# One value run of four units a tile, with loads gated by sums of g

## The chip, the cores and the metric

The kernel runs on one core of a Trainium2 chip. The metric is device time in microseconds of the whole program; the lower the better. The core has five engines with queues of their own: TensorE (PE, matmuls and its weight loads), VectorE (DVE), ScalarE (ACT), GpSimd (POOL) and SyncE (SP, which here only issues DMAs). They run beside one another and wait for each other through semaphores; each takes its own instructions strictly in order, so an instruction that waits holds all behind it.

## The reference: what is computed

Sliding-window attention, then a two-layer MLP on its output:

```
scores = q @ k^T / 8, kept where |i - j| <= 32;  attn = softmax(scores);  x = attn @ v
h = x @ w_in;  g = h * sigmoid(1.702 * h);  out = g @ w_out
```

q, k and v are 8 batches x 8 heads x 576 positions x 64 (float32). x is 4608 tokens x 512, w_in 512 x 2048, w_out 2048 x 512, the output 4608 x 512 float32.

## The kernel before

**Units and tiles.** The 4608 tokens are cut into 36 units of 128 queries and 9 tiles of four units (512 tokens, `t` = 0 to 8). By "tile t" the text means the stretch of `front(t)` and `back(t)`: it does the MLP of units 4t to 4t+3 and, between its groups, the values (x) of units 4t+4 to 4t+7. A unit's queries are rows 128u+32 on; their windows lie in keys 128u to 128u+191, so a unit needs its own keys and the first 64 of the next unit's. `load_kq` and `load_v` (L141, L211) load a unit's queries, keys or values by DMA from POOL, cast to bfloat16; `T_dma` (L235) transposes queries and keys by DMA from SP (`turn(u)` does queries u and keys u+1). Values sit in `ve[u % 9]`; a second copy shifted by 64 rows, `vo`, is put together by two POOL copies (`odd_v`, L222; `spread` calls it). `vo` has five buffers, of which units from 16 on use three.

**Attention of a unit.** `scores` (PE) into two PSUM banks, exp on ACT, `band` (DVE) multiplies by the mask. `values(u, tag)` is 16 matmuls of 65 columns into two banks, four heads each; the 65th column is the sum of the weights. `norm` (L339, L340 on DVE) takes a reciprocal and a product for each bank, or both banks at once for the double bank "t"; `x_T` transposes the normed x into `xT`, by DMA from SP (L352), or on PE (L356) if it is given a bank.

**The MLP of a tile.** Both layers use seven block products in place of eight (a Strassen scheme): sums of blocks of x (`x_sums`), of w_in and w_out (made once) and of g (`g_sums`, four DVE operations per group) are the operands. Layer 1 of a tile is four groups `n` = 0 to 3 (`l1_group`). Each works in the four single banks A, C, B, E: products 1 (into A) and 7 (into C), ACT copies both, products 6 and 2, DVE adds (L484, "the first sum"), products 5 and 4, DVE adds (L490, "the second sum"), product 3; four gelus on ACT (L471) empty the banks. Between the products, `fill(1)`, `fill(7)`, `fill(2)` and `fill(4)` issue matmuls of layer 2 (list `l2`, tiles behind) from the table SHARES; they are what PE does while DVE and ACT work. Product 5 waits for the first sum, product 3 for the second. `side` and `fill(4)` hand DVE the masks and the sums of g of the group before. Layer 2 has its own banks LA and LB.

**Order.** Everything is issued in one hand-written order (`opening`, `run`, then for each tile `front(t)` and `back(t)`); there is no scheduler. `front(t)` does the scores of the four units of tile t+1, the last sums of g and the sums of x of tile t. `back(t)` does tile t's four groups and, between them, the values of tile t+1. With u = 4t+4 the unit that the next tile begins with, `back` before:

- in tile 2: four value runs of one unit, two in front of groups 1 and 3 and two inside them (bank "t" each time);
- in tiles 3 to 7: in front of group 1 the values of u (banks A, C) and u+1 (bank "t"), in front of group 3 those of u+2 and u+3 likewise; norms and the DMA transposes of x follow each run; AHEAD says how many layer-2 matmuls stand around a run;
- in every group: `turn(u+n+4)`, `fetch(u+n+5)` (queries, keys and values of one unit each) and `spread(u+n+2)`, with shifts in tile 3;
- unit 34's x is transposed on PE in `front(8)`, the others by DMA.

The loads have no gate of their own: POOL issues each as soon as it gets there and the buffer is free (five stages each for queries and keys). POOL is slowed by the odd-value copies, which wait for PE's values and for landed loads.

## Time and profile before

| | us |
|---|---|
| median of 3 runs | 281.32 (281.23 to 282.04) |
| the profiled execution, its own time | 281.27 |
| its span (first to last instruction) | 279.5 |
| PE busy | 268.2 (96%) |
| DVE busy | 210.9 (75%) |
| ACT busy | 195.4 (70%) |
| POOL busy | 133.0 (48%) |

Times in the profile are microseconds from the span's start. Lines of code are given as L70 and so on; L70 is the helper that records every matmul, so matmuls are told apart by their tiles: `pv` values, `sc` scores, `h` layer 1, `o` layer 2, `tp` transposes. A row of the timeline gives start, duration, engine, line, operation, tiles written and read, shapes and a count; matmuls are pipelined, so a row's duration is longer than its share of PE, and the distance between starts tells what PE spends. In a row of DMA issues the last number is the median time from issue to landing. The stretches that tiles 2 to 7 take in the trace begin at 78.9 (tile 2's group 0) and, with the scores in `front`, at 100.4, 128.0, 155.7, 183.3 and 210.9; the last layer-2 work ends the program.

### The profile page before, as it was taken

How to read it: one execution, taken by the hardware profiler on the slowest of the kernel's cores; microseconds unless marked ns; L12 is line 12 of the kernel's file. 1: busy time of each engine (PE TensorE's matmuls, PEld its weight loads, DVE VectorE, ACT ScalarE, POOL GpSimd, SP SyncE). 2: the span in 40 equal slices, each digit the busy share in tenths (PEclk: the TensorE clock that was granted, in tenths of full speed). 3: DMA queues.
4: the chain of work that ended last, by engine and by line, in shares of the span. 5: the costliest groups of instructions: out<-in, count | busy, mean ns of one | idle time of the engine just before them, and what ended most of it. 6: DMA issues, size and time to landing. Idle time of an engine off the chain costs nothing.

```text
span 279.5 us, 8854 instructions
## 1 busy us (share of the span) xinstructions
PE 268.2 (96%) x3632; PEld 222.6 (80%) x3632; DVE 210.9 (75%) x491; ACT 195.4 (70%) x343; POOL 133.0 (48%) x199
## 2 busy tenths in 40 slices
PE   1989999999999999999999999999999999999995
PEld 1568656776888888888888888888888888888884
DVE  3454598897997798788888887888778887945731
ACT  2586893989897588758875877687759775568411
POOL 8894695999593554635684519442520100000000
PEclk9999999999999999999999999999999999999999
DMA  8999999999999999999999999999972050202023
GB/s 88 166 204 199 178 207 165 185 136 159 131 167 140 203 120 140 172 189 115 182 194 178 126 163 159 134 183 132 168 91 85 2 115 19 77 2 75 2 104 124
DMA packets 150265, 37.61 MB, mean 135 GB/s; under 512 B 138064, under 2 KB 145872, under 8 KB 150224
## 3 DMA queue, kind: packets, MB, share of 16 engines
q0 software_dynamic: 106656, 18.42, 95.5%
q1 hardware_dynamic: 43120, 18.10, 37.9%
q8 instruction: 28, 0.46, 0.7%
q10 hardware_dynamic: 448, 0.52, 0.6%
q14 instruction: 13, 0.11, 0.1%
HBM read 36.83 MB, written 9.44 MB: 166 GB/s over the span
## 4 chain that ended last, share of the span: by engine, by line
PE 90%; DMA 4%; POOL 3%; ACT 1%; issue 1%; POOLq 0%
PE o L70 41%; PE h L70 39%; PE pv L70 4%; DMA w<-in_moe_w_in_dram 4%; PE sc L70 3%; POOL ve L211 1%; POOL kq L152 1%; PE tp L201 1%; PE tp L244 1%; ACT p L279 1%; POOL w L125 1%; PE tp L368 0%; ACT kq L67 0%; PE tp L356 0%; ACT L692 0%
## 5 line engine op out<-in xcount | busy, mean ns | idle before, releaser
L471 ACT ACTIVATE g<-h 128x512 f16<-128x512 f32 x128 | 72.2, 598 | 35.0 <-PE h L70 34.8
L222 POOL COPY vo<-ve 64x264 int32<-64x264 int32 x71 | 32.7, 461 | 79.3 <-PE pv L70 52.0
L70 PEld LDWEIGHTS <-g 128*128 128x128 f16 x576 | 54.5, 98 | 10.1
L70 PE MATMUL h<-xs,a 128*128 128x256 f16 x384 | 57.6, 272 | 0.0
L70 PEld LDWEIGHTS <-a 128*128 128x128 f16 x512 | 49.5, 98 | 9.1
L70 PE MATMUL o<-w,g 128*128 128x256 f16 (+1 forms) x320 | 55.0, 294 | 0.0
L70 PEld LDWEIGHTS <-w 128*128 128x128 f16 x496 | 47.7, 98 | 7.6 <-DMA w<-in_moe_w_in_dram 0.2
L70 PE MATMUL h<-xT,w 128*128 128x256 f16 (+1 forms) x368 | 53.5, 277 | 0.1
L70 PEld LDWEIGHTS <-gs 128*128 128x128 f16 x384 | 36.7, 98 | 4.7
L70 PE MATMUL o<-b,g 128*128 128x256 f16 x256 | 38.3, 273 | 0.0
L70 PE MATMUL o<-b,gs 128*128 128x256 f16 x256 | 37.7, 273 | 0.0
L484 DVE TENSOR_TENSOR h<-h,s 128x512 f32<-128x512 f32 x32 | 22.4, 699 | 19.8 <-PE h L70 19.1
L211 POOL DMA_DIRECT2D ve<-in_v_dram x40 | 34.3, 864 | 5.6 <-DMA w<-in_moe_w_out_dram 2.1
L279 ACT ACTIVATE p<-sc 128x512 bf16<-128x512 f32 x64 | 32.8, 618 | 1.2 <-PE sc L70 1.0
L67 ACT COPY h<-h 128x512 f32<-128x512 f32 x32 | 18.8, 588 | 16.7 <-PE h L70 16.3
L340 DVE TENSOR_TENSOR x<-pv,rec 128x256 f16<-128x256 f32 (+1 forms) x52 | 27.4, 527 | 1.8
L141 POOL DMA_DIRECT2D qst<-in_q_dram x35 | 28.2, 809 | 0.3
L490 DVE TENSOR_TENSOR h<-h,s 128x512 f32<-128x512 f32 x32 | 22.4, 699 | 6.4 <-PE h L70 6.1
L141 POOL DMA_DIRECT2D kst<-in_k_dram x31 | 26.5, 855 | 0.8 <-DMA w<-in_moe_w_out_dram 0.8
L309 DVE TENSOR_TENSOR p<-p,mask 128x1024 bf16<-128x1024 bf16 x32 | 22.3, 696 | 0.2
L67 ACT COPY s<-h 128x512 f32<-128x512 f32 x32 | 19.2, 600 | 1.2
L70 PE MATMUL h<-xs,w 128*128 128x256 f16 x128 | 19.2, 273 | 0.0
(88 smaller groups left out, 343.2 us busy)
## 6 DMA issues: line engine op xcount, KB each, us to landing
out_dram<-o_sb SPq DMA_DIRECT2D x33, 256.0 KB, 4.6
ve<-in_v_dram POOLq DMA_DIRECT2D x32, 128.0 KB, 6.9
kst<-in_k_dram POOLq DMA_DIRECT2D x25, 128.0 KB, 6.5
qst<-in_q_dram POOLq DMA_DIRECT2D x21, 128.0 KB, 5.6
w<-in_moe_w_out_dram POOLq DMA_DIRECT2D x4, 512.0 KB, 11.0
w<-in_moe_w_in_dram POOLq DMA_DIRECT2D x3, 512.0 KB, 9.9
qst<-in_q_dram POOLq DMA_DIRECT2D x7, 96.0 KB, 5.7
kq<-in_q_dram POOLq DMA_DIRECT2D x2, 256.0 KB, 5.9
```

The costliest lines, as they stand in the source:

```text
L67: (eng.copy if eng is self.nc.scalar else eng.tensor_copy)(out, in_)
L70: self.nc.tensor.matmul(out, lhsT, rhs, start=start, stop=stop, skip_group_check=True)
L125: self.nc.gpsimd.dma_start(self.w1[:, :, lo:lo + n], self.w_in[:, lo:lo + n].rearrange("(k p) f -> p k f", p=128))
L141: self.nc.gpsimd.dma_start(t[off:off + n], src[b, :, s:s + n, :].rearrange("h s d -> s h d"))
L211: self.nc.gpsimd.dma_start(t[off:off + n, :, :self.D], self.v[b, :, s:s + n, :].rearrange("h s d -> s h d"))
L222: eng.tensor_copy(*((words(vo[64:128]), words(self.ve[u % 9][64:128])), (words(vo[0:64]), words(nxt)))[i])
L279: self.nc.scalar.activation(p[:, eo].rearrange("k h s -> k (h s)"), sc[eo], AF.Exp, scale=self.scale)
L309: (eng or self.nc.vector).tensor_mul(pv, pv, msk.to_broadcast([128, 8, 2, SQ]))
L340: dve.tensor_mul(x[:, 4 * at:4 * (at + n), :].rearrange("p (b h) d -> p b h d", b=n), acc[:, :, :, :D], r.to_broadcast([128, n, 4, D]))
L471: act.activation(g[:, f, 256 * half:256 * half + 256], bank.rearrange("p (i n) -> p i n", i=2), AF.Gelu_apprx_sigmoid)
L484: dve.tensor_add(e, b, s7)
L490: dve.tensor_add(c, b, s7)
```

## The change

- **Values and norms.** In tiles 2 to 7 `values_four(u)` does all four units in one run of 64 matmuls in front of group 2. The 32 heads lie one behind the other in five stretches: A (7 heads), E (7, put at the end of the bank, with the first matmul of each half widened over what lies ahead of them), C (4), and the two halves of "t" (7 each). `norm_four` norms A, C and E right behind the run (then the transposes of x of units u and u+1 are issued), one layer-2 matmul goes ahead of group 2, and the halves of "t" are normed in that group's two `side` places, each followed by one transpose of x. x lies in one fixed buffer of four units (`xn`). Groups 1 and 3 have no value run any more; unit 34's x goes by DMA too. All four masks of a tile are handed out from group 0 on.
- **Shares.** SHARES is new and AHEAD is gone; the sum over a tile is the same 112 with `front`, and 64 over tile 2's groups as before.
- **Loads.** Behind groups 2 and 3 of tile 2 and all groups from tile 3 on, as long as there are loads, POOL does a copy of one element of the sums of g (`seen`), of the group before. POOL's loads behind it wait for that sum. In tile 2 queries and keys 17 to 19 come without a gate, values 17 and 18 and queries 20 (keys 21) behind group 2, values 19 and 20 behind group 3. From tile 3's group 2 on each group loads unit u+n+7.
- **Odd values.** Units from 16 on use four `vo` buffers (2, 3, 4, 0 in turn); the copies for u+2 and u+3 are made behind group 0, for u+4 and u+5 behind groups 2 and 3.
- **Transposes of queries and keys.** Tile t issues `turn` u+5 and u+6 in group 0, u+7 in group 1 and u+8 in group 3; tile 3 issues units 20 to 23 in groups 0 and 1 and 24 in group 3, so that keys 24 (in `turn(23)`) are ahead of the four x made in it (units 16 to 19) on SP's queue; tile 2 issues 16 to 19 in groups 0 to 2.

```diff
@@ -94,7 +94,9 @@
         self.v_first = cst.tile([64, self.H, 66], BF16, name="v_first")
         self.ve = [cst.tile([128, self.H, 66], BF16, name=f"ve{i}") for i in range(9)]
         self.vo = [cst.tile([128, self.H, 66], BF16, name=f"vo{i}") for i in range(5)]
+        self.xn = cst.tile([128, 4, self.H, self.D], F16, name="xn")
         self.spark = cst.tile([128, 1], F32, name="spark")
+        self.seen = cst.tile([1, 1], F16, name="seen")
 
     def setup_mask(self):
 
@@ -210,9 +212,12 @@
         for off, b, s, n in list(self.pieces(128 * u, 128))[which]:
             self.nc.gpsimd.dma_start(t[off:off + n, :, :self.D], self.v[b, :, s:s + n, :].rearrange("h s d -> s h d"))
 
+    def odd(self, u):
+        return self.vo[u % 5 if u < 16 else (2, 3, 4, 0)[u % 4]]
+
     def odd_v(self, u, eng, parts=(0, 1)):
 
-        vo = self.vo[u % (3 if u > 15 else 5)]
+        vo = self.odd(u)
         nxt = self.v_first if u == self.NU - 1 else self.ve[(u + 1) % 9][0:64]
 
         def words(ap):
@@ -322,14 +327,14 @@
         for h in range(self.H):
             o = slice((h % 4) * (D + 1), (h % 4 + 1) * (D + 1))
             for blk in range(2):
-                vt = (self.ve[u % 9], self.vo[u % (3 if u > 15 else 5)])[blk]
+                vt = (self.ve[u % 9], self.odd(u))[blk]
                 w = p[:, h % 2, h // 2 * 2 + blk, :] if len(p.shape) == 4 else p[:, h % 2, h // 4, h // 2 % 2, blk, :]
                 self.mm(acc[h // 4][64 * blk:64 * blk + 64, o], w, vt[:, h, :D + 1],
                         start=(h % 4 == 0))
 
     def norm(self, u):
         dve, D = self.nc.vector, self.D
-        x = self.x[u] = self.sb("x", [128, self.H, D], F16, 4)
+        x = self.x[u] = self.xn[:, u % 4]
         rec = self.sb("rec", [128, 2, 4, 1], F32, 3)
         at = 0
         for acc in self.acc.pop(u):
@@ -340,6 +345,42 @@
             dve.tensor_mul(x[:, 4 * at:4 * (at + n), :].rearrange("p (b h) d -> p b h d", b=n), acc[:, :, :, :D],
                            r.to_broadcast([128, n, 4, D]))
             at += n
+
+    FOUR = {"A": 0, "E": 7, "C": 14, "t0": 18, "t1": 25}
+
+    def four(self, tag):
+        return self.FOUR[tag], 4 if tag == "C" else 7, 512 - 7 * (self.D + 1) if tag == "E" else 0
+
+    def values_four(self, u):
+
+        D = self.D
+        p = [self.p.pop(u + i) for i in range(4)]
+        b = {tag: self.bank(tag, name="pv") for tag in "AECt"}
+        self.acc[u] = b | {"t0": b["t"][:, 0], "t1": b["t"][:, 1]}
+        for tag in self.FOUR:
+            lo, n, pad = self.four(tag)
+            for i in range(n):
+                x, h = divmod(lo + i, self.H)
+                at, more = pad + i * (D + 1), pad * (i == 0)
+                for blk in range(2):
+                    vt = (self.ve[(u + x) % 9], self.odd(u + x))[blk].rearrange("p h d -> p (h d)")
+                    self.mm(self.acc[u][tag][64 * blk:64 * blk + 64, at - more:at + D + 1],
+                            p[x][:, h % 2, h // 2 * 2 + blk, :], vt[:, h * (D + 2) - more:h * (D + 2) + D + 1],
+                            start=(i == 0))
+
+    def norm_four(self, u, tags, units):
+
+        dve, D = self.nc.vector, self.D
+        x = self.xn.rearrange("p u h d -> p (u h) d")
+        for tag in tags:
+            lo, n, pad = self.four(tag)
+            acc = self.acc[u].pop(tag)[:, pad:pad + n * (D + 1)].rearrange("p (h e) -> p h e", e=D + 1)
+            r = self.sb("rec4", [128, 7, 1], F32, 3)[:, 0:n]
+            dve.reciprocal(r, acc[:, :, D:])
+            dve.tensor_mul(x[:, lo:lo + n], acc[:, :, :D], r.to_broadcast([128, n, D]))
+        for i in units:
+            self.x[u + i] = self.xn[:, i]
+            self.x_T(u + i)
 
     def x_T(self, u, tag=None, eng=None):
         nc = self.nc
@@ -603,11 +644,8 @@
 
 
 
-    SHARES = {("first", 1): (3, 0, 5, 4), ("first", 2): (0, 6, 6, 6), ("first", 3): (3, 1, 7, 7), ("last", 0): (0, 12, 6, 6),
-              0: (4, 4, 6, 6), 1: (3, 3, 6, 6), 2: (0, 6, 5, 6), 3: (2, 2, 5, 5)}
-
-
-    AHEAD = {1: (0, 6), 3: (2, 3)}
+    SHARES = {("first", 0): (2, 4, 5, 3), ("first", 1): (2, 3, 5, 4), ("last", 0): (0, 12, 6, 6),
+              0: (4, 5, 6, 7), 1: (4, 5, 6, 7), 2: (2, 4, 5, 7), 3: (3, 4, 5, 5)}
 
     def opening(self):
 
@@ -733,13 +771,18 @@
         self.x_T2(6, "t", dve)
         self.do(self.l2, 6)
 
+    def ahead(self, what, *us):
+        for u in us:
+            if "q" in what:
+                self.load_kq("q", u)
+                self.load_kq("k", u + 1)
+            if "v" in what:
+                self.load_v(u)
+
     def fetch(self, u):
         self.load_kq("q", u)
         self.load_kq("k", u + 1)
-        if u < 16:
-            self.load_v(u + 1)
-        elif u >= 18:
-            self.load_v(u - 1)
+        self.load_v(u + 1)
 
     def spread(self, u):
         if 16 <= u < self.NU:
@@ -761,7 +804,6 @@
             self.l2eng = self.nc.scalar
             do(late, 3)
             do(l2, 8)
-            self.x_T(self.NU - 2, "t", self.l2eng)
             xs = self.x_sums(t)
             do(xs, 1)
             do(l2, 12)
@@ -788,60 +830,62 @@
         do, l2 = self.do, self.l2
         u = 4 * t + 4
         bands = [lambda i=i: self.band(u + i) for i in range(4)] if more else []
-        dv = bands[0:2]
+        dv = bands
         for n in range(4):
-            if (t, n) == (3, 1):
-                self.turn(20)
-            if (t, n) != (3, 0):
-                self.turn(u + n + 4)
-            if (t, n) not in ((2, 3), (3, 0), (3, 3)):
-                self.fetch(u + n + 5)
-            if t == 2 and n in (1, 3):
-                self.values(u + n - 1, "t")
-                self.norm(u + n - 1)
-                self.x_T(u + n - 1)
-            elif more and n in (1, 3):
-                do(l2, self.AHEAD[n][0])
-                self.values(u + n - 1, "AC")
-                self.norm(u + n - 1)
-                if u + n < self.NU - 1:
-                    self.x_T(u + n - 1)
-                self.values(u + n, "t")
-                self.norm(u + n)
-                self.x_T(u + n)
-                do(l2, self.AHEAD[n][1])
-            if (t, n) == (3, 0):
-                self.fetch(20)
-            self.spread(u + n + 2)
-            if (t, n) == (3, 0):
-                self.fetch(21)
-            if (t, n) == (3, 3):
-                self.fetch(24)
-
-            key = ("first", n) if t == 2 else ("last", n) if not more else n
+            for i in {2: ((4,), (5,), (6, 7), ()), 3: ((4, 5), (6, 7), (), (8,))}.get(t, ((5, 6), (7,), (), (8,)))[n]:
+                self.turn(u + i)
+            if t == 2:
+                self.ahead("kq", *((17,), (18, 19), (), ())[n])
+            if more and n == 2:
+                self.values_four(u)
+                self.norm_four(u, ("A", "C", "E"), (0, 1))
+                do(l2, 1)
+
+            key = n if more else ("last", n)
+            if t == 2:
+                key = ("first", n) if n < 2 else n
             share = dict(zip((1, 7, 2, 4), self.SHARES.get(key, (3, 3, 5, 5))))
 
             def fill(i):
                 do(l2, share[i])
                 self.l2eng = self.nc.scalar
-                if t == 2 and n in (1, 3) and i == 7:
-                    self.values(u + n, "t")
-                    if n == 3:
-                        self.norm(u + n)
-                        self.x_T(u + n)
-                if i == 4:
-                    do(dv, 2 if (t, n) == (2, 2) else 99)
+                if i == 4 or more and (n, i) == (1, 7):
+                    do(dv, 99 if i == 4 else 2)
 
             def side(i):
-                if (t, n, i) == (2, 1, 0):
-                    self.norm(u + n)
-                    self.x_T(u + n)
+                if more and n == 2:
+                    self.norm_four(u, (f"t{i}",), (2 + i,))
                 else:
                     do(dv, 1)
 
             self.l1_group(t, n, fill, side)
-            dv += bands[2:4] if n == int(t == 2) else []
             dv += self.g_sums(t, 2 * n, 2)
+            if more and (t > 2 or n > 1):
+                if u + n + 7 <= self.NU:
+                    c = 2 * ((n - 1) % 4) + 1
+                    self.nc.gpsimd.tensor_copy(self.seen, self.gs[t - (n == 0)][0:1, 2, c, 255:256])
+                if t == 2:
+                    if n == 2:
+                        self.ahead("v", 17, 18)
+                        self.ahead("kq", 20)
+                    else:
+                        self.spread(16)
+                        self.ahead("v", 19, 20)
+                        self.ahead("kq", 21)
+                    continue
+                if (t, n) == (3, 0):
+                    self.ahead("kq", 22)
+                    self.spread(17)
+                for i in ((2, 3), (), (4,), (5,))[n]:
+                    self.spread(u + i)
+                if (t, n) == (3, 0):
+                    self.ahead("v", 21, 22)
+                    self.ahead("kq", 23)
+                elif (t, n) == (3, 1):
+                    self.ahead("v", 23)
+                    self.ahead("kqv", 24)
+                else:
+                    self.ahead("kqv", u + n + 7)
         return dv
 
     def run(self):
@@ -897,7 +941,7 @@
         self.seed2 = dve
         self.odd_v(14, pool)
         self.odd_v(15, pool)
-        self.fetch(16)
+        self.ahead("kq", 16)
         late = self.back(2)
         for t in range(3, self.NT):
             self.front(t, late)
```

## The prediction

> **What bounds the kernel now.** I read the page's head first, then the busy times by stretch, then TensorE (PE) row by row.
>
> ```profile
> span 279.5 us, 8854 instructions
> PE 268.2 (96%) x3632; PEld 222.6 (80%) x3632; DVE 210.9 (75%) x491; ACT 195.4 (70%) x343; POOL 133.0 (48%) x199
> DMA  8999999999999999999999999999972050202023
> 128.73:156.36 27.63, 27.63 (x385) 23.90 (x386) 23.30 (x55) 20.68 (x37) 16.87 (x26) 1.00 2.30 168
> ```
>
> The last row is tile 4's stretch: length, then PE, PEld, DVE, ACT, POOL. A tile takes 27.63 us and PE is busy in all of it at full clock; only what PE issues, and what it waits for, can move the end. The DMA engines are as full until 75% of the span, so a late transfer is the danger. The profiled execution took 281.27 us, 0.05 under the median of 281.32; I sum against 281.27.
>
> Where PE is not packed shows in the start times. Tile 4's two value runs (its pairs of units), in order of time:
>
> ```profile
> 137.70 0.60 PE L70 MATMUL h<-xT,a 128*128 128x256 f16 x4
> 138.23 0.22 PE L70 MATMUL pv<-ve,p 128*64 128x65 bf16 x1
> 138.28 0.20 PE L70 MATMUL pv<-ve,p 128*64 128x65 bf16 x1
> 138.76 0.19 PE L70 MATMUL pv<-vo,p 128*64 128x65 bf16 x1
> 138.89 0.83 PE L70 MATMUL o<-w,g 128*128 128x256 f16 x6
> 149.96 0.19 PE L70 MATMUL pv<-vo,p 128*64 128x65 bf16 x1
> 150.10 0.19 PE L70 MATMUL pv<-ve,p 128*64 128x65 bf16 x1
> 238.92 0.60 PE L70 MATMUL o<-w,gs 128*128 128x256 f16 x4
> 239.36 0.39 PE L356 MATMUL tp<-identh,x 128*128 128x128 f16 x4
> 239.58 0.60 PE L70 MATMUL o<-w,gs 128*128 128x256 f16 x4
> ```
>
> A 256-column matmul takes 0.11 (four from 238.92 to 239.36). Four from 137.70 end at 138.14, and the run begins at 138.23: entering costs 0.09. Its 32 matmuls start within 0.53, about 0.017 each, with a slow first pair (+0.02). Leaving takes 0.13 from 138.76, 0.11 over one matmul. So one run's changeover costs 0.22. In the second run the ninth matmul comes 0.14 after the eighth (149.96 to 150.10): 0.12 of waiting for bank C. The rest of the tile is back to back but for known waits of 0.04.
>
> **The change, part by part.**
>
> *Values, tiles 3 to 7.* Two runs of 32 become one of 64: the same matmuls, one changeover less (-0.22). The new run takes banks A, E, C, t in turn and reaches C after 28 matmuls (0.48) instead of 8; the wait of 0.12 on C's gelu goes. Two matmuls into E are 57 columns wider: +0.03.
>
> What is late next is the norm. The run lies right before group 2, whose first product writes bank A again, with one layer-2 matmul between.
>
> ```profile
> 138.59 0.18 DVE L339 RECIPROCAL rec<-pv 128x4 f32<-128x4 f32 x1 [0.16 <-PE pv L70]
> 138.81 0.42 DVE L340 TENSOR_TENSOR x<-pv,rec 128x256 f16<-128x256 f32 x1
> 139.93 0.69 DVE L340 TENSOR_TENSOR x<-pv,rec 128x512 f16<-128x512 f32 x1
> 86.61 0.70 DVE L484 TENSOR_TENSOR h<-h,s 128x512 f32<-128x512 f32 x1 [1.36 <-PE h L70]
> 87.22 0.20 DVE L339 RECIPROCAL rec<-pv 128x8 f32<-128x8 f32 x1
> 87.45 0.69 DVE L340 TENSOR_TENSOR x<-pv,rec 128x512 f16<-128x512 f32 x1
> 88.06 0.69 DVE L490 TENSOR_TENSOR h<-h,s 128x512 f32<-128x512 f32 x1
> 88.99 0.42 DVE L67 COPY o<-o 128x256 f32<-128x256 f32 x1
> 89.32 0.41 DVE L67 COPY s7o<-o 128x256 f32<-128x256 f32 x1
> 88.23 0.60 PE L70 MATMUL o<-b,g 128*128 128x256 f16 x4
> 88.80 0.49 PE L70 MATMUL h<-xT,a 128*128 128x256 f16 x3
> ```
>
> The reciprocal starts 0.23 after the start of the bank's last matmul (the eighth, about 138.36, to 138.59). Bank A now has 14: last start 0.25, reciprocal at 0.48, 0.20 long (0.18 for 4, 0.20 for 8), a gap of 0.04, and a product of 448 elements, 0.62 between the rows of 256 (0.42) and 512 (0.69): 1.34, with 0.05 until PE goes on (88.06+0.69 to 88.80) 1.39. PE is there after 64x0.017=1.09, 0.11 to leave and 0.11 for one matmul: 1.31. Wait: +0.08.
>
> In the same group the t bank's first norm lies between the group's two sums on DVE, as a norm lies in tile 2 above: there the sums start 1.45 apart (86.61, 88.06), and PE with four matmuls of cover (88.23) waits 0.13 (88.67 to 88.80). New: 0.61 to the reciprocal, 0.20+0.04+0.54 for the norm (a product's end overlaps the next by 0.08), and layer 2's own 256-element sum, 0.33 as between 88.99 and 89.32: 1.72 apart, 0.27 more, against seven matmuls of cover, 0.33 more: +0.07. The second t norm and the four sums of g end before group 3 needs DVE.
>
> Per tile -0.22-0.12+0.03+0.08+0.07 = -0.16; five tiles **-0.8**. Bounds: both waits gone, -0.31 a tile; one 256-element step (0.33) more ahead of each, +0.50. I take the middle: DVE's order around the run is the one worked out.
>
> *Tile 2.* Four runs of one unit become one: -3x0.22, +0.03+0.08+0.07. Its group 0 loses cover: three layer-2 matmuls ahead of the last product, five now.
>
> ```profile
> 82.52 0.70 DVE L490 TENSOR_TENSOR h<-h,s 128x512 f32<-128x512 f32 x1
> 83.30 0.38 PE L70 MATMUL h<-xT,a 128*128 128x256 f16 x2
> ```
>
> With two fewer that product would come at 83.08, but the sum ends at 83.22: +0.19. Group 1 keeps four, and its 0.13. Sum **-0.3**.
>
> *Unit 34's x by DMA, not PE.* Four transposes less, 239.36 to 239.58: **-0.2**. Its ACT copy goes too, beside other work. Its transpose is issued in group 2, one group and 4 us before it is read.
>
> *Loads, gates, odd values.* POOL gains 16 one-element copies; each holds the loads behind it until a sum of g is done. Data for a tile then still lands a tile ahead of its scores (the q, k loaded behind group 0 are transposed in group 1 and read in the next tile), so I cost the holding itself at nothing; where that cover is thin is the next part. New in tiles 4 to 7: four odd-value copies now open on the last sum of g, just where DVE makes the sums of x.
>
> ```profile
> 128.78 0.42 DVE L412 TENSOR_TENSOR gs<-g 128x512 f16<-128x512 f16 x1
> 129.05 0.42 POOL L222 COPY vo<-ve 64x264 int32<-64x264 int32 x1
> 129.23 0.51 DVE L413 TENSOR_TENSOR g<-g 128x512 f16<-128x512 f16 x1
> ```
>
> The sum that began inside a POOL copy took 0.51, not 0.42; the one that began first took 0.42. Three sums stand ahead of product 6, 0 to 0.27 late at 0.09 each; that product gets one layer-2 matmul more of cover (0.11), so PE waits 0 to 0.16. I take +0.03 in each of four tiles, near the low end, since only sums that begin inside a copy are lengthened: **+0.1**. [...]
>
> *x of tile 3 behind keys 24.* On SP, queries 23 and keys 24 are now transposed ahead of the four x made in tile 3 (units 16 to 19, summed in front of tile 4), and they are loaded late: on POOL behind the odd values of unit 19, which wait for values 20, loaded after the gate in tile 2's group 3.
>
> ```profile
> ve<-in_v_dram POOLq DMA_DIRECT2D x32, 128.0 KB, 6.9
> kst<-in_k_dram POOLq DMA_DIRECT2D x25, 128.0 KB, 6.5
> L211 POOL DMA_DIRECT2D ve<-in_v_dram x40 | 34.3, 864 | 5.6 <-DMA w<-in_moe_w_out_dram 2.1
> 123.78 2.51 SPq L352 DMA_TRANSPOSE xT<-x  x2
> 156.08 0.43 DVE L415 TENSOR_TENSOR gs<-g,gs 128x512 f16<-128x512 f16 x1
> 155.66 0.70 PE L70 MATMUL sc<-qT,kT 64*64 64x64 bf16 x48
> 133.00 0.43 DVE L400 TENSOR_TENSOR xs<-xT 128x512 f16<-128x512 f16 x1 [0.40 <-DMA xT<-x]
> 133.77 0.60 PE L70 MATMUL h<-xs,a 128*128 128x256 f16 x4
> DMA to landing us min/median/max: 4.6/5.3/7.8
> DMA to landing us min/median/max: 4.3/6.8/9.4
> ```
>
> The last rows are x's transposes in 100 to 164 us and the q, k transposes in 100 to 130. Now the last x is issued at 125.0, lands by 133.0 and is 0.40 late for DVE, hidden from PE. New, step by step: the gate opens with the last sum of g of tile 2's group 2. In tile 4 that sum ends at 156.51, 0.85 behind the next scores (155.66); two tiles of 27.63 earlier and 0.3 gained, 100.9. Unit 16's odd copies (0.9), then values 19 and 20, issued by 102.7 and landed 6.9 later, 109.6. Until 109.9 POOL issues q21, k22, q22, k23 (0.86 each, an estimate of 1.4 in two pieces) and copies for units 17 and 18; unit 19's are done by 110.8; v21, v22 and q23 bring k24's issue to 114.0, landed 120.5. Its transpose and a store (1.3, and 0.8 by estimate) last to 122.6; three x (1.26 each) put the last issue at 126.4, landed at 131.7 to 134.2. It is needed by 133.77 less 0.48 for the sum and 0.46 gained by then: 132.8. Wait 0 to 1.4; a landing near the middle, 133.0, gives 0.2 and the longer tail speaks for a little more: **+0.3**. With values 20 and keys 24 at 9.4 it is 4.
>
> Sum: -0.8-0.3-0.2+0.1+0.3 = -0.9: **280.4 us**.
>
> **Rivals.** *Slower: tile 3's x (above).* It decides alone: gains without it are 1.2, so a wait of 2.0 passes +0.3% (0.84 us, about what a measurement here can tell from no change). For it: loads that bunch up behind gates, the 9.4 of the row above; against it: the idle DMA that the gates leave before. At a wait of 3: 283.1.
>
> [...]
>
> *No change.* The changeovers are saved and DVE takes them back: at one of the two places in each of six tiles it is 0.2 later than worked out, as when a POOL copy holds one of its steps: 280.4+1.2=281.6. For it: neither place has cover left; against it: DVE idles in between.
>
> *More.* x lands in time and the two waits on DVE vanish, -0.31x5-0.4-0.2: 279.1. For it: DVE is busy in 23.30 of 27.63; against it: both waits are chains of dependent steps, not a full engine.
>
> **How the numbers follow.** Forecast 0.42 (its own range 279.8 to 280.7), more 0.10, no change 0.23, x of tile 3 0.18, lock 0.07. The bound of 0.3% lies at 280.5, inside the forecast's own range: four fifths of it (0.34) and all of *more* make 0.44 faster; the rest of the forecast and *no change* 0.31 the same; the two slower ones 0.25. The range of 279.2 to 282.8 leaves out the lock, the far end of tile 3's x and the edge of *more*.
>
> **What would show it.** In the changed profile: one run of 64 values a tile, PE's first product 0.2 after it, no wait inside it; tile period 27.4 to 27.5 from tile 4 on; sums of x without DMA waits except in front of tile 4; no transposes at the end. It is wrong if PE idles in the layer-1 groups behind DVE's norms, if the run waits for odd values or values, or if tile 4's first group waits for x.

## The result, and the profile after

The changed kernel takes 288.4 us (median of 6 runs, 287.13 to 289.32) against 281.39 for the kernel before on the same chip (281.23 to 282.22): 1.0238 times, with a 95% interval of 1.0207 to 1.0269. The forecast was 280.4, in a range of 279.2 to 282.8. The profiled execution took 289.32, the longest of the six; its mean granted clock was 0.982, that of the other five 0.988. In the runs below, executions more than 1.5% above the fastest of their kernel (two of ten in each of two runs) are left out of medians, ratios and intervals.

The page of the changed kernel: its span, and the slices of PE and of its granted clock.

```profile
span 287.6 us, 8849 instructions
PE   1989999999999999994799999999999999999994
PEclk9999999999999999998589999999999999999999
```

PE has a hole in slices 19 and 20 (129 to 144 us), and its clock falls there. Everything else is packed as before. The next two fences cut both kernels into tiles, from the first scores of one to those of the next: length, PE, PEld, DVE, ACT, POOL, and then the granted clock (third number from the end). First the kernel before, for tiles 2, 3, 4 and for 7 with the tail, then the changed kernel for the same, with tile 5 and a stretch inside tile 4.

```profile
65.94:100.39 34.45, 34.45 (x568) 27.86 (x567) 28.17 (x66) 27.09 (x49) 20.42 (x30) 1.00 1.87 160
100.39:128.03 27.64, 27.64 (x386) 23.98 (x385) 23.51 (x57) 20.59 (x36) 16.88 (x24) 1.00 1.54 153
128.03:155.66 27.63, 27.63 (x385) 23.90 (x384) 23.30 (x56) 20.68 (x37) 16.87 (x26) 1.00 2.28 168
210.94:275.85 64.91, 64.91 (x728) 57.35 (x728) 44.65 (x106) 38.96 (x72) 0.81 (x2) 1.00 0.19 56
```

```profile
65.66:99.81 34.15, 34.12 (x568) 27.87 (x568) 29.03 (x70) 26.86 (x49) 16.42 (x24) 1.00 1.67 148
99.81:127.22 27.41, 27.41 (x385) 23.89 (x384) 23.08 (x54) 20.77 (x37) 22.54 (x36) 1.00 2.11 140
127.22:164.16 36.94, 31.20 (x385) 25.43 (x384) 22.70 (x54) 20.94 (x37) 15.06 (x26) 0.86 1.44 156
164.16:191.58 27.42, 27.42 (x385) 23.88 (x385) 22.70 (x54) 20.78 (x37) 16.43 (x28) 1.00 1.68 154
219.00:283.47 64.47, 64.47 (x724) 57.03 (x724) 44.27 (x104) 38.55 (x71) 0.00 (x0) 1.00 0.18 59
136.03:145.40 9.37, 7.41 (x35) 5.00 (x36) 3.56 (x8) 3.04 (x4) 1.15 (x2) 0.51 1.72 186
```

Tile 2 gains 0.30, tile 3 0.23, tiles 5 and 6 0.22 each, tile 7 with the tail 0.44. Tile 4 alone takes 36.94, where 27.42 stood to be had: +9.52. What it waits for stands in its timeline (start, duration, engine, line, operation; in brackets the idle time and its releaser):

```profile
131.66 0.60 PE L70 MATMUL o<-w,g 128*128 128x256 f16 x4
136.03 1.01 PE L70 MATMUL h<-xT,w 128*128 128x256 f16 x4 [3.77 <-DMA xT<-xn]
136.84 1.06 PE L70 MATMUL o<-w,g 128*128 128x256 f16 x4
139.86 1.03 PE L70 MATMUL h<-xs,a 128*128 128x256 f16 x4 [1.96 <-DVE xs L441]
...
139.38 0.43 DVE L441 TENSOR_TENSOR xs<-xT 128x512 f16<-128x512 f16 x1 [7.58 <-DMA xT<-xn]
```

By the starts (four matmuls from 131.66 end at 132.1, four from 136.84 at half clock at 137.7) PE idles 3.9 for the first transposed x of tile 3 and 2.2 for the sum of x behind the last. Then it runs at half clock: in the stretch of 9.37 the granted clock is 0.51, and four matmuls take 0.83 (136.03 to 136.84) instead of 0.44. That is the rest, 3.4.

The queues that lead to it, from the same timeline, and then, by tile, the landing of keys 24 (issue to landing in us) and the four transposes of x (durations of the issues in ns, first and last start, landing):

```profile
109.70 3.84 POOL L227 COPY vo<-ve 64x264 int32<-64x264 int32 x6
115.71 0.91 POOL L143 DMA_DIRECT2D qst<-in_q_dram  x1
116.59 0.92 POOL L143 DMA_DIRECT2D kst<-in_k_dram  x1
...
124.49 1.19 SPq L240 DMA_TRANSPOSE kT<-kst  x1
125.79 1.00 SPq L546 DMA_DIRECT2D out_dram<-o_sb  x2
126.89 6.84 SPq L393 DMA_TRANSPOSE xT<-xn  x4
```

```profile
DMA to landing us min/median/max: 7.9/7.9/7.9
...
L393 SPq DMA_TRANSPOSE xT<-xn x4: 1188/1398/2206, 126.9 to 132.5; - x4
DMA to landing us min/median/max: 6.7/6.8/7.6
```

Queries 23 are issued at 115.7 and land at 123.0, keys 24 are issued at 116.6 and land at 124.4. SP stands still for the queries from 118.5 to 123.0, and 0.2 more for the keys, with x behind; the first x is issued at 126.9, the last at 132.5, and lands at 139.3.

### The profile page after: what moved, and what is told of

It reads as the page before. It is cut to its first block, busy times and chain, and to the rows that moved or that the text cites. A ratio compares the mean times of both kernels' runs of the same rounds, so it can differ in the third digit from the quotient of the medians.

```text
span 287.6 us, 8849 instructions
## 1 busy us (share of the span) xinstructions
PE 270.0 (94%) x3628; PEld 223.6 (78%) x3628; DVE 210.2 (73%) x483; ACT 195.4 (68%) x342; POOL 136.3 (47%) x215
## 4 chain that ended last, share of the span: by engine, by line
PE 90%; DVE 3%; DMA 2%; ACT 2%; issue 1%; POOL 1%; SPq 0%; POOLq 0%; DVEq 0%
PE o L70 40%; PE h L70 39%; PE sc L70 4%; PE pv L70 4%; DMA xT<-xn 2%; PE tp L179 1%; PE tp L203 1%; PE tp L249 1%; POOL kq L154 1%; ACT p L284 1%; ACT p L305 1%; DVE xn L345 1%; PE tp L409 0%; PE tp L397 0%; ACT kq L67 0%
## 5 line engine op out<-in xcount | busy, mean ns | idle before, releaser
L70 PEld LDWEIGHTS <-g 128*128 128x128 f16 x576 | 55.9, 99 | 10.5
L70 PE MATMUL h<-xs,a 128*128 128x256 f16 x384 | 58.7, 276 | 2.0 <-DVE xs L441 2.0
L70 PEld LDWEIGHTS <-a 128*128 128x128 f16 x512 | 50.2, 99 | 12.5 <-DVE xs L441 2.4
L70 PE MATMUL h<-xT,w 128*128 128x256 f16 (+1 forms) x368 | 54.5, 281 | 3.9 <-DMA xT<-xn 3.8
L70 PE MATMUL o<-w,g 128*128 128x256 f16 (+1 forms) x320 | 56.2, 296 | 0.0
L70 PE MATMUL o<-b,gs 128*128 128x256 f16 x256 | 40.2, 275 | 0.0
L213 POOL DMA_DIRECT2D ve<-in_v_dram x40 | 34.2, 866 | 5.3 <-DMA w<-in_moe_w_out_dram 2.1
L866 POOL COPY seen<-gs 1x1 f16<-1x1 f16 x16 | 3.2, 199 | 54.4 <-DVE gs L456 54.3
L67 ACT COPY o_sb<-o 128x256 f32<-128x256 f32 (+1 forms) x23 | 10.7, 464 | 12.6 <-PE o L70 12.6
```

The source lines that it names most:

```text
L67: (eng.copy if eng is self.nc.scalar else eng.tensor_copy)(out, in_)
L70: self.nc.tensor.matmul(out, lhsT, rhs, start=start, stop=stop, skip_group_check=True)
L213: self.nc.gpsimd.dma_start(t[off:off + n, :, :self.D], self.v[b, :, s:s + n, :].rearrange("h s d -> s h d"))
L866: self.nc.gpsimd.tensor_copy(self.seen, self.gs[t - (n == 0)][0:1, 2, c, 255:256])
```

## The experiments

The first four asked which part makes x late: the order on SP, the late loading of keys 24, the gates, or the clock. All times were taken beside the kernel before (281.16 for the first four, 281.3 for the next, 281.39 for the last two).

**Keys 24 behind x on SP.** Queries 23 and keys 24 are transposed after the four x.

```diff
-  3: ((4, 5), (6, 7), (), (8,))
+  3: ((4, 5), (6,), (), (7, 8))
```

> The changed kernel with one edit: in tile 3 the transposes of queries 23 and keys 24 are issued behind the four x, in group 3, not ahead of them. Theory (SP's order holds the x of tile 3 until keys 24 have landed): x lands by about 130 us, the wait of 3.9+2.3 us in tile 4's group 0 goes, and with it the 3.3 us of half-speed matmuls behind it. Keys 24 themselves then land at 131 to 133 and the last scores of tile 4's front, at 130, wait 1 to 2.5 us. Expected 280.5 to 282.5 (without any wait 279.8). Rival (the DMA engines are simply overloaded in tile 3, in whatever order): x still lands near 137 to 139 and the time stays at 286 to 289.

It took 289.06 (1.0266, 1.0227 to 1.0305). The wait in front of tile 4 is now:

```profile
PE sc L70 <- DMA qT<-qst: 3.8, 1, 3.8
```

x is no longer waited for: its four transposes, issued from 118.5 to 123.6, have landed by 131.9. The scores in front of tile 4 wait for queries 23, as long as PE did for the first x before. So the time is near the rival's range, but not by its mechanism, and the order on SP alone isn't it: PE stands still from 130.6 for the queries here, and from 132.1 for x in the changed kernel; both are wanted within 2 us. The queries, issued right behind x at 125.6, took 8.8 to land.

**Keys 24 loaded first.** Queries 23 and keys 24 are loaded ahead of the odd-value copies and of values 21 and 22.

```diff
                 if (t, n) == (3, 0):
-                    self.ahead("kq", 22)
+                    self.ahead("kq", 22, 23)
                     self.spread(17)
...
                     self.ahead("v", 21, 22)
-                    self.ahead("kq", 23)
```

> The changed kernel with one edit: in tile 3's group 0 POOL issues the loads of queries 23 and keys 24 right behind queries 22, ahead of the odd-value copies of units 17 to 19 and of values 21 and 22. SP's order is as in the changed kernel. Theory (keys 24 are late because POOL waits for values 20 before it issues their load): their load is issued at about 111.5 in place of 116.6, x is issued from about 122 to 126 and lands by 132.5; wait in tile 4's group 0 of 0 to 0.7, no half-speed stretch. Expected 279.6 to 280.8. Rival (overloaded DMA): keys 24 land little earlier, the wait shrinks by 1 to 3 us only, 283 to 287.

It took 283.35 (1.0076, 1.0046 to 1.0106; 283.8 over all ten executions): about 5 won, but still slower than before, and in the rival's range, not in the one expected. The four x (count, durations, first and last start) and their landings, in the stretch 118 to 136:

```profile
L393 SPq DMA_TRANSPOSE xT<-xn x4: 1237/1282/1672, 122.8 to 127.2; - x4
DMA to landing us min/median/max: 7.1/8.3/9.2
```

They are issued 4 to 5 us earlier, nearly where the prediction had them (last at 126.4), and then take 7.1 to 9.2 to land, not 5.3 to 7.8. There is a second cause.

**PE kept busy.** 62 unread matmuls stand in front of the two products of tile 4's group 0 that wait (36 and 26); nothing reads their results, so they are added work and nothing else.

```diff
+        def idle_work(bank, count):
+            if (t, n) == (4, 0):
+                for _ in range(count):
+                    self.mm(bank[:, 0:256], self.w1[:, 0, 0:128], self.w1[:, 0, 0:256], start=True)
+        idle_work(a, 36)
...
+        idle_work(c, 26)
```

> The changed kernel with 62 matmuls of 128x256 more that nobody reads, in tile 4's group 0: 36 into bank A ahead of product 1 and 26 into bank C ahead of product 7, so that PE works while it would wait for x. The output is the same. Theory (the clock halves because PE stands idle for 3.9 us; the half speed, 3.3 us over some 10 us, comes on top of the wait): granted clock 1.0 throughout, x lands as late as before, 285 to 286. Rival (the half clock has another cause, such as time or load): the half-speed stretch stays and the time is 288 to 290.

It took 286.58 (1.019, 1.0172 to 1.0209), 0.6 above the range expected and below the rival's. Tile 4 in it:

```profile
127.27:161.55 34.28, 34.28 (x447) 29.88 (x446) 22.68 (x54) 20.94 (x37) 15.09 (x26) 1.00 1.56 155
```

62 matmuls of 0.109 are 6.8, and 27.42 + 6.8 = 34.2: the added work fills the wait, x is as late as it was, and the clock stays at 1.00. Tile 4 is 2.7 shorter though PE has 0.7 more to do than it had to wait. So the half clock comes from PE's standing still, and it costs 3.3 in the profiled execution of the changed kernel. By the medians (288.4 and 286.58) it is nearer 2.5, as that execution was the longest of six.

**No gates.** The one-element copies are left out; POOL issues loads as soon as it gets there.

```diff
-                if u + n + 7 <= self.NU:
-                    c = 2 * ((n - 1) % 4) + 1
-                    self.nc.gpsimd.tensor_copy(self.seen, self.gs[t - (n == 0)][0:1, 2, c, 255:256])
```

> The changed kernel without the 16 one-element copies on POOL that hold the loads behind sums of g; all else, the order of loads included, is as in the changed kernel. Theory (holding the loads of tile 2 is what makes keys 24 late): values 17 on are issued from 83 us, keys 24 some 8 to 13 us earlier, no wait for x in tile 4: 279.6 to 280.8. Rival (the DMA engines could not have moved them earlier): keys 24 still land after 121 and the time stays over 284. Second rival (without gates loads collide with x's transposes in each tile): small waits for x in several tiles, 281 to 283.

It took 285.49 (1.0149, 1.011 to 1.0188), a miss; the first rival's "over 284" came true. Keys 24 are issued at 108.4, 8 earlier, but take 13.2 and land at 121.6, only 2.8 earlier. x is late in front of tile 3 already, in the starts of PE there, and less late in tile 4; the length of tile 3 stands last:

```profile
106.33 0.60 PE L70 MATMUL h<-xT,w 128*128 128x256 f16 x4 [1.66 <-DMA xT<-xn]
108.99 0.61 PE L70 MATMUL h<-xs,a 128*128 128x256 f16 x4 [1.61 <-DVE xs L441]
...
99.64:130.82 31.18, 27.91 (x386) 23.66 (x385) 22.79 (x54) 20.95 (x37) 21.83 (x33) 1.00 2.00 159
```

With the gates POOL issues no load from 83.1 to 97.2 us, without them seven between 92.1 and 98.3; the four transposes of tile 2's x (issued from 93.8 to 97.7 with the gates) land in 2.5 to 6.1 us with them and in 8.2 to 9.6 without, at nearly the same time, and tile 3 takes 31.18 for 27.41, 3.8 more. But the gates push the same loads into tile 3. That pointed to the number of transfers beside x. The next four tried it.

**Loads of 25 to 28 later.** Keys 24 are loaded first as above, and loads behind them are put off. By the edit, queries 24 (with keys 25), units 25 and 26 and values 27 each go one group later; queries 27 and unit 28 stay in their groups, so the expectation below says more than was done.

```diff
                 if (t, n) == (3, 0):
                     self.ahead("v", 21, 22)
                 elif (t, n) == (3, 1):
-                    self.ahead("v", 23)
-                    self.ahead("kqv", 24)
+                    self.ahead("v", 23, 24)
+                elif (t, n) == (3, 2):
+                    self.ahead("kq", 24)
+                elif (t, n) == (3, 3):
+                    self.ahead("kqv", 25)
+                elif (t, n) == (4, 0):
+                    self.ahead("kq", 26, 27)
+                    self.ahead("v", 26)
+                elif (t, n) == (4, 1):
+                    self.ahead("kq", 28)
+                    self.ahead("v", 27, 28)
```

(In tile 4 the transposes of unit 26 go with those of 27 in group 1.)

> Edit: as in the run with keys 24 loaded ahead of values 21 and 22, and the loads of units 25 to 28 of tiles 3 and 4 are each issued one or two groups later (queries 24 and keys 25 in group 2, unit 25 in group 3, 26 to 28 in tile 4), so that fewer transfers lie beside the transposes of x of tile 3. Theory that the DMA engines are full in tile 3 because the loads of 25 and 26 were moved into it: the transposes of x land 5 to 6 us after their issue instead of 7 to 9, tile 4 takes 27.4 to 28 us and the time is 279.5 to 280.8. Rival, that the x are late by their place in the queue and the distance alone, whatever lies beside them: they still land after 135, tile 4 takes over 30 us, and the time is 282 or more. If the loads put off are missed in their turn, tile 5 waits, and the time is 281 to 284.

It took 280.06 (0.9955, 0.9935 to 0.9974): faster than the kernel before. The four x of tile 3 and their landings, then tiles 4 and 5:

```profile
L393 SPq DMA_TRANSPOSE xT<-xn x4: 1198/1202/1267, 121.4 to 125.7; - x4
DMA to landing us min/median/max: 5.4/5.6/5.6
```

```profile
127.55:154.97 27.42, 27.42 (x386) 23.91 (x386) 22.78 (x54) 20.78 (x37) 17.54 (x28) 1.00 2.22 156
154.97:183.45 28.48, 27.77 (x386) 23.74 (x385) 22.78 (x54) 20.86 (x37) 16.64 (x28) 1.00 1.82 163
```

Issued at nearly the same times as in the run with keys 24 loaded first (122.8 to 127.2 there), the same transposes land in 5.4 to 5.6 instead of 7.1 to 9.2. Tile 4 has no wait left; about 1 us has moved to tile 5, for the x of tile 4.

**The same, with values 17, 18 and queries 20 not held.** The gate in tile 2's group 2 is left out.

```diff
-                if u + n + 7 <= self.NU:
+                if u + n + 7 <= self.NU and (t, n) != (2, 2):
```

> Edit: the one before, and the one-element copy that holds values 17, 18 and queries 20 in tile 2's group 2 is left out, so that these loads are issued near 83 us, in the 13 us in which the DMA queue of POOL is idle. Theory that the capacity of the DMA engines in tiles 2 to 4 is the limit: 128 KB pieces that go into the idle stretch make values 20 and keys 24 land earlier by up to 3 us, no wait in tile 4, 279.5 to 280.8, 0 to 1 less than without the edit. Rival, that the held loads then collide with the x of tile 2 (issued 88 to 97): front 3 starts later than 100.2 and the time is 281 or more.

It took 280.16 (0.9947, 0.9922 to 0.9973), the same as without the edit. Neither the gain of up to 1 us came nor the collision: keys 24 were issued at 110.9, no earlier than at 110.6 without it, and tile 3 began at 99.9 in both.

**The kernel before, with 24 to 26 loaded earlier.** Nothing of the change; only more loads beside x of tile 3, as the change has them (called the crowd below).

```diff
-            if (t, n) not in ((2, 3), (3, 0), (3, 3)):
+            if (t, n) not in ((2, 3), (3, 0), (3, 3), (4, 0), (4, 1)):
                 self.fetch(u + n + 5)
...
-            if (t, n) == (3, 3):
+            if (t, n) == (3, 2):
                 self.fetch(24)
+            if (t, n) == (3, 3):
+                self.fetch(25)
+                self.fetch(26)
```

> Edit on the kernel before, nothing else changed: the loads of units 24, 25 and 26 are issued one group or more earlier, in tile 3's groups 2 and 3, as far ahead as the changed kernel has them. Theory that asking the DMA engines for those units in tile 3 is by itself enough to make the transposes of x late: in the kernel before x of tile 3 lands 0.4 after its sum could start, so with latencies 2 to 4 us longer tile 4's first group waits 2 to 4 us, and the time is 282 to 286. Rival, that only the order of the changed kernel (gates, values 20 and keys 24 one behind the other) makes x late: 281.0 to 281.8.

It took 283.0 in the median of eight executions (280.86 to 284.22; 1.005, 1.0018 to 1.0081; 283.54 over all ten). Its last two x of tile 3 and their landings, in the third row the landings of the same two in the kernel before, and then tile 4:

```profile
L352 SPq DMA_TRANSPOSE xT<-x x2: 1204/1701/2198, 123.7 to 126.0; - x2
DMA to landing us min/median/max: 9.7/9.9/10.2
...
DMA to landing us min/median/max: 5.0/6.4/7.8
```

```profile
127.99:158.44 30.45, 28.16 (x385) 23.74 (x384) 23.20 (x56) 20.84 (x37) 14.34 (x22) 1.00 1.80 150
```

Issued where the kernel before issues them (123.8 and 125.1), they take 9.7 to 10.2 instead of 5.0 and 7.8, and tile 4 is 2.8 longer. The loads are slower too: values issued between 116 and 132 us took 11.2 to land, against 7.3. The crowd can make x late by itself, without gates and without the new order. It doesn't each time: executions of 280.86 and 281.5 are no slower than the kernel before.

**The value run alone.** `values_four`, its norms, SHARES and four `vo` buffers with the order of loads and transposes of the kernel before, and no gates. (The diff is the change's first half.)

> Edit: the value run of four units, its norms, the shares of layer 2 and the fourth odd-value buffer of the changed kernel, with the loads, transposes and their order as in the kernel before and no one-element copies. It tells what the value run is worth apart from the loads. By the prediction's steps: five tiles at -0.2, tile 2 -0.3, unit 34's x -0.2, hence 279.5 to 280.2 if nothing waits for loads; up to 281.5 if the single run of tile 3, which now needs unit 19's odd values at 115.8, waits for values 20. Rival, that DVE takes the changeovers back in the single run: 281.0 to 281.8 with a tile period of 27.6.

It took 291.92 (1.0352, 1.0303 to 1.04), slower than anything else here and far outside every range expected. In front of tile 4, the four x on SP, the transpose of queries 23 behind them, and the scores that read it:

```profile
119.99 5.64 SPq L393 DMA_TRANSPOSE xT<-xn  x4
126.15 1.25 SPq L240 DMA_TRANSPOSE qT<-qst  x1
...
134.15 0.24 PE L70 MATMUL sc<-qT,kT 64*64 64x64 bf16 x2 [1.91 <-DMA qT<-qst]
```

The same stands in front of tiles 3, 5 and 6: SP issues the transposes of the last unit's queries and keys right behind the four x, which are now made in one run (97.4, 157.2 and 188.4 for the queries), and they land 6.7 to 7.9 us later, when the scores have begun to wait. In these stretches SP waits for no load. POOL does stand at odd-value copies for up to 14.6 us, but in total no longer than in the kernel before (48.8 against 52.0). So the new order isn't an extra: the single run needs those transposes ahead of x, as the change has them in group 1. That was read from the trace and not tried alone. This run doesn't give the price of the value run by itself, which I had hoped for.

**Later loads alone.** On the changed kernel, only those later loads; queries 23 and keys 24 stay behind values 21 and 22.

```diff
                 if (t, n) == (3, 0):
-                    self.ahead("kq", 22, 23)
+                    self.ahead("kq", 22)
...
                     self.ahead("v", 21, 22)
+                    self.ahead("kq", 23)
```

(against the run at 280.06)

> Edit on the changed kernel: only the loads of units 25 to 28 are put off as in the run at 280.06; queries 23 and keys 24 stay where the change has them, behind values 21 and 22. With the changed kernel (288.4), keys 24 ahead alone (283.8) and both edits (280.06) it makes a table of two by two. Theory that the number of loads beside the transposes of x is one half of the cause and the late keys 24 the other: keys 24 land near 122.5, the last x is issued near 128.5 and lands at 134 to 135, tile 4's first group waits 1.5 to 2.5 us at full clock, 281.3 to 283.0. Rival, that the crowd of loads alone does it: no wait, 279.8 to 280.6. Rival, that the late keys 24 alone do it: over 3 us of wait and the half clock behind it, 285 or more.

It took 286.77 (1.0187, 1.015 to 1.0224), in the second rival's range and not in the theory's. Its four x:

```profile
L393 SPq DMA_TRANSPOSE xT<-xn x4: 1206/1236/2192, 126.0 to 131.3; - x4
DMA to landing us min/median/max: 5.8/6.5/8.3
```

That closes the table of two by two (medians, us):

| | loads of 24 to 27 as in the change | later |
|---|---|---|
| keys 24 behind values 21, 22 | 288.4 | 286.8 |
| keys 24 ahead of them | 283.35 | 280.06 |

The late keys 24 cost about 5 or 6.7, the crowd 1.6 or 3.3. I expected two halves; the keys' place is the larger part, and the crowd counts for more once they are in time. With the same later loads, x issued about 5 us later took 5.8 to 8.3 instead of 5.4 to 5.6: late transposes are issued into the later loads. In the profiled execution here x isn't earlier at all: PE goes on behind the last wait at 140.1, in the changed kernel at 139.9. What is shorter is the slow clock, which ends near 142.8 instead of 145.4. So the differences in the table hold the slow clock as well as the waits, and the two causes don't simply add.

**Values 28 and 29 later.** On the run at 280.16, to take away the wait in tile 5.

```diff
                 elif (t, n) == (4, 1):
                     self.ahead("kq", 28)
-                    self.ahead("v", 27, 28)
+                    self.ahead("v", 27)
+                elif (t, n) == (4, 2):
+                    self.ahead("v", 28)
+                    self.ahead("kq", 29)
+                elif (t, n) == (4, 3):
+                    self.ahead("v", 29)
+                    self.ahead("kqv", 30)
```

> Edit on the run at 280.16: values 28 and 29 are loaded one group later in tile 4, away from the transposes of x made in tile 4, for which tile 5's first group still waits 0.29 at one place. If that wait is the last one that loads cause, tile 5 takes 27.42 instead of 27.73 and the time is 279.4 to 280.2; if values 28 are then late for the odd values of unit 27, the value run of tile 5 waits and the time is 280.3 to 281.

It took 280.35 (0.9962, 0.9934 to 0.9989), above the range expected. Tile 5 is 27.42, as expected; but in this execution tile 4 waits 0.8 for an x that was in time in the run it is built on, with the same order up to there. The last of those x is issued at 127.2 here and at 126.1 there; executions of this one kernel lie between 279.38 and 282.91, and these three kernels can't be told apart.

## Why the prediction was wrong, point by point

**Values, tiles 3 to 7: right, a little better.** -0.22 a tile against -0.13 (-0.16, and +0.03 for POOL's copies). The two waits that were worked out are there. In tile 4's stretch, where the clock is back at 1.00, before group 2 and in it:

```profile
153.67 0.19 PE L70 MATMUL pv<-vo,p 128*64 128x65 bf16 x1
153.80 0.28 PE L70 MATMUL o<-b,gs 128*128 128x256 f16 x1
154.00 0.61 PE L70 MATMUL h<-xT,w 128*128 128x256 f16 x4
158.30 0.49 PE L70 MATMUL o<-b,g 128*128 128x256 f16 x3
158.69 0.60 PE L70 MATMUL h<-xT,a 128*128 128x256 f16 x4
...
156.24 0.70 DVE L525 TENSOR_TENSOR h<-h,s 128x512 f32<-128x512 f32 x1 [0.97 <-PE h L70]
157.95 0.69 DVE L531 TENSOR_TENSOR h<-h,s 128x512 f32<-128x512 f32 x1
```

The run's last matmul starts at 153.67 and PE goes on at 153.80, as it left a run before (0.13). The one matmul of cover ends at 153.91, group 2's first product starts at 154.00: 0.09 of waiting for bank A's norm (0.08 foreseen). The two sums of group 2 start 1.71 apart (1.72 foreseen), and PE waits 0.06 behind three matmuls that end at 158.63 (0.07 foreseen). The 0.09 a tile by which it came out better is in part POOL's copies, whose 0.03 doesn't show; the rest wasn't traced to a place.

**Tile 2: right.** -0.30 forecast, 34.45 to 34.15 measured. **Unit 34's x: right.** The last stretch is 0.44 shorter; if tile 7 gains 0.22 like the others, 0.22 is left for the four transposes (0.2 forecast).

**POOL's odd copies: the rival at 0.07, the lock, fell.** It had each of three sums wait for a whole POOL copy (0.42), by which the tiles would be 1.15 longer; tiles 5 and 6 are 27.42. Sums do lie beside the copies: in tile 6 three of them, from 196.7 on beside four copies, took 0.65, 0.51 and 0.51 instead of 0.42, and PE didn't wait. The most is 0.23 more, not a whole copy.

**Holding of loads costed at nothing: wrong in both directions.** Without the gates tile 3 loses 3.8: they hide something. And what they hold comes down in tile 3 beside the x there, with units 24 to 26, which the kernel before loads two groups later. Between 113 and 121 us POOL issues nine loads, in the kernel before four. The prediction looked only at whether each load lands before it is read.

**x of tile 3 behind keys 24, +0.3 (0 to 1.4): the step that failed.** The chain was the right one, and it was named as the one rival that decides alone; its size was wrong. The gate opened as reckoned (100.8 for 100.9). Then values 20 landed at 112.0 for 109.6, as the odd copies of unit 16 had first to wait 1.3 for values 17, and as the load took 7.8 for 6.9; the six copies ended at 113.5 for 110.8; keys 24 were issued at 116.6 for 114.0 and took 7.9 for 6.5: 124.4 for 120.5. Their transpose and the stores let x begin at 126.9 for 122.6; the four x are issued within 5.6 instead of 3.8, as one issue takes up to 2.2 us, and put the last at 132.5 for 126.4. It landed at 139.3 for 133.0. Each term was taken at the kernel before's median, while the change itself put more transfers into just that stretch: the latencies were not a constant to be carried over. The forecast wait was 0.3, the measured ones 3.9 and 2.2, 6.1 in all. The row that allowed "4 if values 20 and keys 24 are at 9.4" was the better end.

**The half clock, not in the sum at all: 3.3.** The rival's price (a wait of 3 gives 283.1) counted a wait as time only. The sum of what was measured, in the profiled execution: 0.28 less in the opening, whose order isn't changed, -0.30, -0.23 in tile 3, +9.31 in tile 4 (36.94 for 27.63), -0.22 twice and -0.44 make 7.6 at the last matmul; the last stores add 0.5: 8.1, the difference of the spans (287.6 and 279.5).

**Without that step the forecast stands.** With keys 24 first and the loads spread out, the same value run gives 280.06 and 280.16, where the sum without x of tile 3 would have been 280.1. That they agree to 0.1 is in part luck: the terms of the value run and of unit 34 came out at -1.6 where the forecast had -1.2 with POOL's copies, and waits such as those left in tile 5 take the rest back.

## What to carry to other kernels

When a change reorders loads, write down for each stretch what transfers lie in it before and after, and take the latencies of the crowded rows where the crowd grows; a median of the old trace holds only for the old crowd (x here: 5.4 to 5.6 us, or 7.1 to 9.2 with more loads beside it). Follow the last item of a queue through every landing ahead of it, and let no transposes that the next tile needs at once stand behind a load that was itself put last, or right behind a batch of others. If a wait of some microseconds on PE is possible, price the slow clock behind it too (here 3.3 us behind waits of 3.9 and 2.2).

## What the runs showed of the hardware

**The clock after a wait.** In the changed kernel PE stood still for 3.9 and 2.2 us, and the granted clock was 0.51 over 9.4 us; with the same late x and PE kept busy it was 1.00. In the run with keys 24 behind x a wait of 3.8 had 0.50 behind it, from 134.5 to 140. In the profiled executions, waits of 1.8 and 1.8 within 4.5 us left it at 1.00 (the run with no gates), and so did 1.6 and 0.9 (the kernel before with early loads). But two of the four executions with no gates had a mean clock of 0.988. And in the run of the value run alone waits of 2.0 and 0.4 within 2.5 us brought it down, and later 0.7 and 1.4 within 2.1 us (0.78 over 164 to 168 us). The stretch right behind the first of these, with the clock third from the end:

```profile
134.00:138.00 4.00, 3.62 (x41) 2.70 (x42) 1.47 (x4) 1.08 (x2) 2.87 (x4) 0.69 1.84 243
```

The waits of 2.0 and 0.4, and of 0.7 and 1.4, add up to 2.4 and 2.1, less than the 1.8 and 1.8 that left the clock at 1.00, and the clock still fell. Next to these waits PE did only scores, 64x64 matmuls; whether that is the reason no run here shows.

**Latency of transposes by what lies beside them.** The same four SBUF-to-SBUF transposes of x, issued within 2 us of the same time, landed in 5.4 to 5.6 us or in 7.1 to 9.2, and two of them in the kernel before in 5.0 and 7.8 or in 9.7 and 10.2, by whether about one or two units of queries, keys and values more were being loaded beside them or just ahead of them.
